# The last tile's second layer: from two interleaved halves to three parts in sequence, the middle one stored by ScalarE

## The chip, the core and the metric

The kernel runs on one core of one Trainium2 chip. The metric is the device time of one execution in microseconds, less is better. The profile names the engines PE (TensorE matmul), PEld (TensorE weight load), DVE (VectorE), ACT (ScalarE), POOL (GpSimd) and SP (SyncE). A name with a small q behind it (SPq, ACTq, PEldq) is that engine's sequencer, which issues DMAs, waits on semaphores and takes branches.

## What is computed

A sliding-window attention with four sink keys, followed by layer normalisation and a two-layer MLP with a residual. There are 4 sequences of 768 positions and 8 heads of 64, so that the MLP sees 3072 rows of 512 columns; its hidden layer has 2048 columns.

```python
scores = scale * np.matmul(q, k.transpose(0, 1, 3, 2))
keep = is_sink | in_window            # 4 sinks, window of 128
a = softmax(np.where(keep, scores, -1e9))
x = np.matmul(a, v)                   # heads side by side: 3072 x 512
xn = (x - mu) / np.sqrt(var + 1e-06) * g_ln
out = x + np.maximum(xn @ w_ch1, 0.0) @ w_ch2
```

## The kernel before

The 3072 rows are 24 tiles of 128 rows (`NT` = 24), and two tiles make a chunk (`NC` = 12 chunks). Attention is computed tile by tile; the MLP chunk by chunk, in `mlp(c)`. Its first layer makes 16 hidden blocks of 128 x 256 for the chunk: 8 PSUM banks' worth of matmuls on line 1045, each bank released by a ReLU on line 1055 that writes bf16 into `h`. The second layer takes the chunk's two tiles in turn (the loop over `i`, line 1061). For one tile it adds up 16 matmuls on line 1074 in one PSUM bank (`pc`): the stationary operand is a 128 x 128 block of `h`, the moving operand a block of `w2`. VectorE then multiplies the bank by the row's inverse deviation and adds `x` (line 1082, SCALAR_TENSOR_TENSOR, written to `ot`), and a DMA stores `ot` (line 1086).

Nothing in the code issues an instruction at once. `P.op(name, engines, priority, emit, ...)` puts each step in a plan with an estimated cost and a priority; `Plan.run` lays the steps out, taking on each engine, among those that can start first, the one of the lowest priority number (ties go to the one that was put in first). The steps are then emitted in the order of their planned start, and each engine works through its own in that order. So the priority on line 1078 sets the order of the matmul groups. The banks are a ring too: `pc` takes one of four single banks ("one").

Tile 23, the last, is cut into two halves of 256 columns (`parts` = 2, line 1065): each has its own bank, its own SCALAR_TENSOR_TENSOR and its own store. The groups of four matmuls have priorities `T + 4*i + s + 2*f + 0.5`: for the halves f = 0 and f = 1 these are 4.5, 5.5, 6.5, 7.5 and 6.5, 7.5, 8.5, 9.5 above T. So the first group of the second half goes between the third and the last group of the first half: the first half is complete after 20 matmuls, not 16.

Behind the last tile stands the end of the program. A flag made from the row sums has been written to SBUF (line 1120); each engine loads it into a register (line 1150, TENSOR_LOAD) and branches on it (line 1151, COMPARE_BRANCH) past the code of a general fallback, `general`, which is not run here. Then each engine reports with a DRAIN (line 1186), SP after it has waited for every store; when all have reported, GpSimd clears the semaphores, and the program ends.

Of the kernel before, what the change touches and what calls it, by code (L numbers as in the profile page):

```python
# [196 lines left out]
def pe(us):  # L197
    return {"PE": (us, us + Plan.PE_DRAIN)}


def act(n):
    t = 0.065 + 0.000833 * n
    return (t, t + 0.105)


def dve(n, per=1.04):
    t = 0.067 + 0.001 * per * n
    return (t, t + 0.09)
# [16 lines left out]
SW_Q = (0.25, 0.7, 0.9)  # L225

LOW, HIGH = 1e-9, 1e9
NEG = -1e30
NEVER = -1e9
BIG = 3.3e38  # L230
# [138 lines left out]
def kernel(  # L369
# [19 lines left out]
    DM = moe_w_ch1.shape[0]  # L389
# [3 lines left out]
    NT = B * RB  # L393
# [8 lines left out]
    P = Plan()  # L402
# [104 lines left out]
    def negs(e):  # L507
        V.tensor_scalar(neg[:, 0:5:2], upper.unsqueeze(1).to_broadcast([128, 3, 128]), -1.0, -NEG, op0=ALU.add, op1=ALU.mult)
        V.tensor_scalar(neg[:, 1:5:2], upper.unsqueeze(1).to_broadcast([128, 2, 128]), NEG, None, op0=ALU.mult)
        V.memset(neg[0:NS, 0:2], 0.0)  # L510
# [37 lines left out]
    for c in range(4):  # L548
        sl = slice(512 * c, 512 * (c + 1))
# [477 lines left out]
    def mlp(c):  # L1027
        T = 16.0 * c + 8.0
        xnt = xnt_b[c]
        h1 = []  # L1030
        by_tile = c < PAR["by_tile"]
        for u in range(NH1 // 2):
            ph, hb = Buf(f"ph{c}_{u}", "one"), Buf(f"h{c}_{u}", "h1")

            def mm_t(e, u=u, ph=ph):
                for s in range(4):
                    for j in range(NDM):
                        nc.tensor.matmul(ph.t[:, 128 * s:128 * s + 128], lhsT=w1[u // 2][:, j, 128 * s:128 * s + 128],  # L1038
                                         rhs=xnt.t[:, j, 128 * (u % 2):128 * (u % 2) + 128], start=j == 0, stop=j == NDM - 1)

            def mm(e, u=u, ph=ph):
                for s in range(2):
                    ht = 2 * u + s
                    for j in range(NDM):
                        nc.tensor.matmul(ph.t[:, 256 * s:256 * s + 256],  # L1045
                                         lhsT=w1[ht // 4][:, j, 128 * (ht % 4):128 * (ht % 4 + 1)],
                                         rhs=xnt.t[:, j, :], start=j == 0, stop=j == NDM - 1)
            pr = T + u + 0.5
            o = P.op(f"ph{c}_{u}", pe(0.944 if by_tile else 0.872), pr, mm_t if by_tile else mm, reads=[xnt_t[2 * c + u % 2] if by_tile else xnt, (Bw1 if c < PAR["x_by_dma"] else Bw1g)[u // 2]],
                     writes=[ph], hold=[hb, xnt])  # L1050
            last_use[u // 2] = [o]

            def rl(e, ph=ph, hb=hb):
                if e == "ACT":
                    nc.scalar.activation(hb.t, ph.t, AF.Relu)  # L1055
                else:
                    V.tensor_scalar_max(hb.t, ph.t, 0.0)
            P.op(f"rl{c}_{u}", {"ACT": act(512), "DVE": dve(512)}, pr - 3, rl, reads=[ph], writes=[hb])
            h1.append(hb)
        T += 8  # L1060
        for i in range(2):
            t = 2 * c + i
            b, r = t // RB, t % RB
            ot, st, rs, x = Buf(f"ot{t}", "ot"), xst_b[t], xst_b[t, "rs"], x_b[t]
            parts = 2 if t == NT - 1 else 1
            wd = DM // parts
            for f in range(parts):
                pc = Buf(f"pc{t}{f}", "one")
                sl = slice(wd * f, wd * (f + 1))
                for s in range(4):  # L1070
                    def mm(e, s=s, i=i, pc=pc, sl=sl, wd=wd):
                        for ii in range(4):
                            ht = 4 * s + ii
                            nc.tensor.matmul(pc.t[:, 0:wd],  # L1074
                                             lhsT=(h1[2 * s + i].t[:, 128 * ii:128 * ii + 128] if by_tile else
                                                   h1[ht // 2].t[:, 256 * (ht % 2) + 128 * i:256 * (ht % 2) + 128 * i + 128]),
                                             rhs=w2[s][:, ii, sl], start=ht == 0, stop=ht == NH1 - 1)
                    P.op(f"pc{t}{f}_{s}", pe(0.865 / parts), T + 4 * i + s + 2 * f + 0.5, mm,
                         reads=[*([h1[2 * s + i]] if by_tile else h1[2 * s:2 * s + 2]), Bw2[s]], **({"writes": [pc]} if s == 0 else {"rw": [pc]}))
                oo = Buf(f"oo{t}{f}")  # L1080
                P.op(f"o{t}{f}", {"DVE": dve(wd, 1.14)}, T + 4 * i + 3.5, lambda e, sl=sl, pc=pc, wd=wd, ot=ot, st=st, x=x:
                     V.scalar_tensor_tensor(ot.t[:, sl], in0=pc.t[:, 0:wd], scalar=st.t[:, 16:17],  # L1082
                                            in1=x.t[:, sl], op0=ALU.mult, op1=ALU.add),
                     reads=[pc, st, rs, x], writes=[ot, oo])
                P.op(f"st{t}{f}", {"SP": (0.54, 0.59)}, T + 4 * i + 3.6,
                     lambda e, sl=sl, ot=ot, b=b, r=r: (nc.sync if e == "SP" else nc.scalar).dma_start(
                         out[b, 128 * r:128 * (r + 1), sl], ot.t[:, sl]),
                     reads=[ot, oo], dma=HW_S)
# [13 lines left out]
    for c in range(NC):  # L1102
        mlp(c)
        if c == PAR["x_by_dma"] - 1:
            for s in range(4):
                for j in range(NDM):
                    P.op(f"w1g{s}{j}", {"DVE": fix(0.26), "ACT": act(512)}, 16.0 * c + PAR["w1g"] + 2 * s + 0.1 * j,
                         lambda e, s=s, j=j: V.tensor_scalar_mul(w1[s][:, j, :], w1[s][:, j, :], gt[:, j:j + 1]) if e == "DVE" else
                         nc.scalar.mul(w1[s][:, j, :], w1[s][:, j, :], gt[:, j:j + 1]),  # L1109
                         reads=[Bw1[s], Bc["gt"]], writes=[Bw1g[s]], after=last_use[s])  # L1110
# [15 lines left out]
    t = PAR["t0"]  # L1126
    for o in order:
# [6 lines left out]
        if n > 0:  # L1134
            free = [(max([e_ for b_, e_ in banks[i].lives if b_ < t], default=0.0), i) for i in range(8)
                    if all(e_ < t or b_ > o.start + 0.3 for b_, e_ in banks[i].lives)]
            if free:
                i = min(free)[1]
                sizes = [512] * (n // 2) + [256] * (n % 2) if cold else [256] * n
                items.append((t + 0.001, -1, (sizes, pairs[i // 2][:, i % 2, :] if i < 4 else ones[i - 4])))  # L1140
        t = o.start + occ * (2 if cold and not o.name.startswith("pm") else 1)
# [49 lines left out]
```

## Time and profile before

| what | value |
|---|---|
| runs | 216.91, 217.95 and 217.96 us, median 217.95 us |
| the profiled execution | 217.75 us, of which 216.3 us is the span from the first to the last instruction |
| granted TensorE clock, mean | 0.997 |
| PE busy | 95% of the span |
| last ReLU of the first layer ends | 205.28 us after the span's start |
| last three SCALAR_TENSOR_TENSOR start | 208.35, 210.65 and 211.86 us |
| last three stores issued by SP | 209.13, 211.16 and 212.37 us |

All times in profile rows count from the start of the span. 1.45 us of the profiled execution lie outside it. Of the span, 3.9 us lie behind the issue of the last store: in that stretch no engine computes.

### The profile page before, as it was taken

The numbers are of one execution on the slowest core, as the hardware profiler recorded it, in microseconds if no ns is written. First come the engines' busy times: TensorE is split into PE (matmuls) and PEld (weight loads), VectorE is DVE, ScalarE is ACT, GpSimd is POOL, SyncE is SP. The second block draws the span as 40 slices with busy tenths as digits, with TensorE's granted clock in tenths as the row PEclk, the third lists the DMA queues.
The fourth block names the chain that finished last, engine by engine and source line by source line (L and its number), as shares of the span: only waits on it lengthen the run. The fifth ranks groups of instructions, "written<-read, shape, count | busy, mean of one in ns | idle before, by whom it ended". The sixth has DMA issues, their size and how long they took to land.

```text
span 216.3 us, 6653 instructions
## 1 busy us (share of the span) xinstructions
PE 206.4 (95%) x2741; PEld 144.5 (67%) x2763; DVE 115.3 (53%) x315; ACT 110.1 (51%) x178; POOL 111.2 (51%) x166
## 2 busy tenths in 40 slices
PE   8898999999999999999999999999999999999991
PEld 2567875755865865865865865865856856856761
DVE  4689875698365356356266366266266266262021
ACT  3795497395652652652652652652652652622600
POOL 7978632499881980970970980971961021020000
PEclk9999999999999999999999999999999999999998
DMA  5999999999999899999998999999999202203011
GB/s 158 187 190 208 191 207 190 189 155 138 161 186 179 113 142 129 116 147 155 121 137 136 122 138 146 116 148 132 129 126 140 73 11 68 73 7 118 0 55 58
DMA packets 104557, 28.07 MB, mean 130 GB/s; under 512 B 94788, under 2 KB 101576, under 8 KB 104520
## 3 DMA queue, kind: packets, MB, share of 16 engines
q0 software_dynamic: 69872, 13.18, 87.5%
q1 hardware_dynamic: 33592, 13.87, 36.2%
q10 hardware_dynamic: 1056, 0.52, 0.9%
q8 instruction: 23, 0.38, 0.8%
q14 instruction: 14, 0.11, 0.2%
HBM read 27.43 MB, written 6.29 MB: 156 GB/s over the span
## 4 chain that ended last, share of the span: by engine, by line
PE 86%; DVE 5%; DMA 4%; issue 2%; ACT 1%; ACTq 0%; DVEq 0%
PE one L1074 37%; PE one L1045 36%; PE pair L979 3%; DMA natf<-in_q_dram 3%; DMA xnt<-xc 2%; PE one L952 2%; PE one L959 2%; PE one L968 1%; DVE st L880 1%; DVE xnt L908 1%; PE one L987 1%; PE one L1038 1%; DVE x L872 1%; PE pair L604 1%; PE pair L729 1%
## 5 line engine op out<-in xcount | busy, mean ns | idle before, releaser
L1074 PE MATMUL one<-w,h 128*128 128x512 bf16 (+1 forms) x378 | 84.5, 370 | 2.2 <-issue 1.4
L1055 ACT ACTIVATE h<-one 128x512 bf16<-128x512 f32 x93 | 55.6, 598 | 46.9 <-PE one L1045 42.6
L1045 PE MATMUL one<-xnt,w 128*128 128x256 bf16 x704 | 79.3, 273 | 0.0
L1045 PEld LDWEIGHTS <-w 128*128 128x128 bf16 x704 | 68.6, 98 | 10.4
L1074 PEld LDWEIGHTS <-h 128*128 128x128 bf16 x400 | 37.3, 98 | 39.6
L997 ACT ACTIVATE pe<-pair 128x768 bf16<-128x768 f32 x36 | 27.2, 808 | 41.0 <-PE pair L979 41.0
L644 POOL DMA_DIRECT2D vn<-in_v_dram x59 | 38.7, 701 | 9.2 <-DMA w<-in_moe_w_ch_dram 6.8
L889 POOL TENSOR_SCALAR st<-st 128x1 f32<-128x1 f32 x24 | 8.4, 350 | 63.5 <-DVE st L882 62.9
L1020 DVE RECIPROCAL rec<-one 128x4 f32<-128x4 f32 x36 | 6.4, 178 | 62.0 <-PE one L968 50.5
L1082 DVE SCALAR_TENSOR_TENSOR ot<-one,st,x 128x512 f32<-128x512 f32 (+1 forms) x25 | 18.2, 727 | 13.9 <-PE one L1074 9.0
L890 POOL TENSOR_TENSOR st<-st,mhalf 128x1 f32<-128x1 f32 x24 | 16.8, 701 | 2.0
L880 DVE BATCH_NORM_STATS2 st<-x 128x6 f32<-128x512 bf16 x24 | 16.7, 695 | 0.8
L702 POOL DMA_DIRECT2D nat<-in_k_dram x16 | 14.9, 934 | 2.6 <-DMA natp<-in_q_dram 1.5
L1022 DVE TENSOR_TENSOR x<-one,rec 128x256 bf16<-128x256 f32 x36 | 15.3, 424 | 1.2
L702 POOL DMA_DIRECT2D nat<-in_q_dram x16 | 14.3, 908 | 0.0
L1002 DVE TENSOR_TENSOR pe<-pe,band 128x768 bf16<-128x768 bf16 x24 | 12.3, 552 | 0.0
L884 DVE TENSOR_SCALAR xc<-x,st 128x512 bf16<-128x512 bf16 x24 | 8.9, 370 | 0.9
L979 PE MATMUL pair<-qT,kT 64*64 64x128 bf16 (+1 forms) x528 | 9.2, 204 | 0.0
L952 PEld LDWEIGHTS <-pe 128*128 128x128 bf16 (+1 forms) x144 | 6.2, 97 | 2.9 <-issue 0.8
L777 ACT ACTIVATE pe<-pair 128x1024 bf16<-128x1024 f32 (+1 forms) x8 | 7.1, 916 | 1.8 <-PE pair L729 1.4
L1038 PE MATMUL one<-xnt,w 128*128 128x128 bf16 x128 | 8.0, 219 | 0.0
L979 PEld LDWEIGHTS <-kT 64*64 64x64 bf16 x528 | 7.2, 108 | 0.4 <-ACT w L1109 0.4
(110 smaller groups left out, 167.0 us busy)
## 6 DMA issues: line engine op xcount, KB each, us to landing
out_dram<-ot SPq DMA_DIRECT2D x23, 256.0 KB
w<-in_moe_w_ch_dram POOLq DMA_DIRECT2D x8, 512.0 KB, 14.0
nat<-in_k_dram POOLq DMA_DIRECT2D x16, 128.0 KB, 4.6
nat<-in_q_dram POOLq DMA_DIRECT2D x16, 128.0 KB, 5.6
vn<-in_v_dram POOLq DMA_DIRECT2D x44, 32.0 KB, 6.0
vn<-in_v_dram POOLq DMA_DIRECT2D x15, 64.0 KB, 5.7
natp<-in_k_dram POOLq DMA_DIRECT2D x3, 256.0 KB, 6.5
vn<-in_v_dram POOLq DMA_DIRECT2D x6, 128.0 KB, 9.2
```

Source lines behind the costliest of these rows:

```text
L644: P.op(f"vld{t}_{i}", {"POOL": (0.8, 0.85)}, prio + 0.001 * i, lambda e, p0=p0, n=n, hs=hs, src=src: G.dma_start(m.t[p0:p0 + n, hs, 0:64], ...
L702: lambda e, nat=nat, ap=ap: G.dma_start(nat.t, ap), writes=[nat], dma=SW, after=gate(c))
L880: P.op(f"bn{t}", {"DVE": fix(0.60)}, d + 0.12, lambda e: V.bn_stats(st.t[:, 8:14], x.t), reads=[x], writes=[st, mv])
L890: G.tensor_tensor(st.t[:, 16:17], st.t[:, 17:18], mhalf, op=ALU.pow)),
L979: nc.tensor.matmul(pps[u].t[64 * g:64 * g + 64, h2, col + c0:col + c0 + n], lhsT=kt.t[rs, hp, k0:k0 + 64], rhs=qT.t[rs, hp, q0:q0 + n], st ...
L997: nc.scalar.activation(pes[j].t.rearrange("p a b -> p (a b)")[:, 0:768].rearrange("p (a b) -> p a b", a=2), pps[j].t[:, :, 0:384], AF.Exp, ...
L1002: V.tensor_mul(at_s, at_s, band[j] if r > 1 else edge[r][j].unsqueeze(1).to_broadcast([128, 4, 192]))
L1022: P.op(f"x{t - 1}{u}", {"DVE": dve(256)}, d + 0.051 + 0.002 * u, lambda e, u=u, rc=rc, pv=pv: V.tensor_tensor(x.t[:, 256 * u:256 * u + 256 ...
L1045: nc.tensor.matmul(ph.t[:, 256 * s:256 * s + 256], lhsT=w1[ht // 4][:, j, 128 * (ht % 4):128 * (ht % 4 + 1)], rhs=xnt.t[:, j, :], start=j ...
L1055: nc.scalar.activation(hb.t, ph.t, AF.Relu)
L1074: nc.tensor.matmul(pc.t[:, 0:wd], lhsT=(h1[2 * s + i].t[:, 128 * ii:128 * ii + 128] if by_tile else h1[ht // 2].t[:, 256 * (ht % 2) + 128 ...
L1082: V.scalar_tensor_tensor(ot.t[:, sl], in0=pc.t[:, 0:wd], scalar=st.t[:, 16:17], in1=x.t[:, sl], op0=ALU.mult, op1=ALU.add),
```

## The change

The last tile's 512 columns are cut at 256 and 384: three parts, of 256, 128 and 128 columns, each with its own bank, VectorE instruction and store. The groups get priorities that are four apart from part to part, so that the parts no longer interleave (4.5 to 7.5, 8.5 to 11.5, 12.5 to 15.5 above T), and planned costs that follow the width. The store of the part for which `len(cuts) - f` is 3 may only go to ScalarE: with four cuts that is f = 1, the middle part. Tiles 0 to 22 have two cuts and one part, for which that number is 2: they stay as they were, with SP as the only issuer.

```diff
+LAST_CUTS, LAST_ACT = (0, 256, 384, 512), (3,)
...
-            parts = 2 if t == NT - 1 else 1
-            wd = DM // parts
-            for f in range(parts):
-                pc = Buf(f"pc{t}{f}", "one")
-                sl = slice(wd * f, wd * (f + 1))
+            cuts = LAST_CUTS if t == NT - 1 else (0, DM)
+            for f in range(len(cuts) - 1):
+                pc, wd = Buf(f"pc{t}{f}", "one"), cuts[f + 1] - cuts[f]
+                sl = slice(cuts[f], cuts[f + 1])
...
-                    P.op(f"pc{t}{f}_{s}", pe(0.865 / parts), T + 4 * i + s + 2 * f + 0.5, mm,
+                    P.op(f"pc{t}{f}_{s}", pe(0.865 * wd / DM), T + 4 * i + s + 4 * f + 0.5, mm,
...
-                P.op(f"st{t}{f}", {"SP": (0.54, 0.59)}, T + 4 * i + 3.6,
+                P.op(f"st{t}{f}", {"ACT" if len(cuts) - f in LAST_ACT else "SP": (0.54, 0.59)}, T + 4 * i + 3.6,
```

## The prediction

> **What bounds the kernel now.** I read the page first, then the chain of waits over the last 26 us, then the timeline of the last 11 us, then the sequencers' instructions of lines 1150, 1151 and 1186, and last the DMA queues in short windows. From the page:
>
> ```profile
> PE 206.4 (95%) x2741; PEld 144.5 (67%) x2763; DVE 115.3 (53%) x315; ACT 110.1 (51%) x178; POOL 111.2 (51%) x166
> ```
>
> The kernel is a stream of matmuls, and the change doesn't touch it before the last tile. So only the tail counts. Its chain (start, duration, what) and its timeline:
>
> ```profile
> 197.59 6.99 PE one L1045 x64
> ...
> 211.86 0.48 DVE ot L1082
> ```
>
> ```profile
> 208.35 0.75 DVE L1082 SCALAR_TENSOR_TENSOR ot<-one,st,x 128x512 f32<-128x512 f32 x1 [2.61 <-PE one L1074]
> ...
> 210.65 0.48 DVE L1082 SCALAR_TENSOR_TENSOR ot<-one,st,x 128x256 f32<-128x256 f32 x1 [1.54 <-PE one L1074]
> ```
>
> ```profile
> 211.16 0.33 SPq L1086 DMA_DIRECT2D out_dram<-ot  x1
> ```
>
> ```profile
> 212.37 0.62 SPq L1086 DMA_DIRECT2D out_dram<-ot  x1
> ```
>
> VectorE follows PE at once, and the last store is issued 0.03 us after the last VectorE instruction (211.86 + 0.48 = 212.34). From there the span has 3.9 us left, and nothing in them computes. What they are is seen in the sequencers' rows (engine, instruction, count: duration in ns min/median/max, first to last start):
>
> ```profile
> L1150 ACTq TENSOR_LOAD <-flag x1: 472/472/472, 205.8 to 205.8; - x1
> ```
>
> ```profile
> L1150 PEldq TENSOR_LOAD <-flag x1: 748/748/748, 209.6 to 209.6; - x1
> ```
>
> ```profile
> L1151 ACTq COMPARE_BRANCH  x1: 50/50/50, 206.3 to 206.3; - x1
> ...
> L1151 ACTq EVENT_SEMAPHORE  x1: 17/17/17, 208.8 to 208.8; - x1
> ...
> L1151 PEldq COMPARE_BRANCH  x1: 3622/3622/3622, 210.5 to 210.5; - x1
> ...
> L1151 SPq COMPARE_BRANCH  x1: 58/58/58, 213.0 to 213.0; - x1
> ```
>
> ```profile
> L1186 POOLq EVENT_SEMAPHORE  x4: 17/17/17, 215.5 to 216.1; - x4
> ...
> L1186 SPq DRAIN  x3: 7/7/13, 215.4 to 215.7; - x3
> ...
> L1186 PEldq DRAIN  x2: 8/8/8, 214.3 to 215.8; - x2
> ```
>
> ```profile
> SPq L1186 <- DMA out_dram<-ot: 1.0, 1, 1.0
> ```
>
> The program ends when every engine has reported with its first DRAIN of line 1186. SP is last, at 215.4, after 1.0 us of waiting for a store; GpSimd goes on at 215.5 and the span ends at 216.3. The second to report is PE, at 214.3: its branch, taken at 210.5, holds it for 3.6 us. So whatever the store gains, the end comes forward by no more than 215.4 - 214.3 = 1.1 us unless PE's branch moves too. That is 0.5% of the kernel, about what a measurement of it can tell from no change.
>
> Why SP waits so long is in the DMA queues, in the windows 213.4 to 214.1 and 214.1 to 214.75 (queue: packets, MB, share of 16 engines):
>
> ```profile
> q1 hardware_dynamic: 135, 0.12, 51.0%
> q14 instruction: 1, 0.01, 5.4%
> ```
>
> ```profile
> q14 instruction: 1, 0.01, 4.5%
> q1 hardware_dynamic: 9, 0.01, 4.3%
> ```
>
> Most of the last store's packets are through by 214.1; a last nine (a sixteenth of 144) move only then, next to a code read on q14. I read this as one DMA engine's slice of the store standing behind the code that engines fetch after their branch.
>
> **The change part by part.** PE first. One matmul of 256 columns takes 6.99 / 64 = 0.109 us (line 1045 above). For 128 columns with a weight load each, line 1038 in the chain of waits has the price, and what PE still had before it when its sequencer loaded the flag is in the groups from 209.92 on:
>
> ```profile
> 25.29 1.79 PE one L1038 x32
> ```
>
> ```profile
> L1074 PE MATMUL one<-w,h 128*128 128x256 bf16 x17 | 2.0, 273 | 0.0
> ```
>
> 1.79 / 32 = 0.056 us. The tile costs 16 x 0.109 + 32 x 0.056 = 3.53 us in place of 32 x 0.109 = 3.49: +0.04. Counted from tile 22's VectorE start at 208.35, part one is complete at 210.10 (before: after 20 matmuls, 210.53, seen as 210.65 on VectorE), part two at 210.99, part three at 211.89 (before 211.86).
>
> The weak spot is the weight load:
>
> ```profile
> L1074 PEld LDWEIGHTS <-h 128*128 128x128 bf16 x49 | 4.7, 98 | 2.2
> ```
>
> A load lasts 98 ns, longer than a matmul of 128 columns; line 1038 has such a load for each matmul and still goes at 56 ns, so I take 56 and keep 98 as the upper bound (a rival). The Trainium skill, "TensorE: Matmul & The Clock Gate", section "Back-to-back issue gap", gives about 81 ns for a sustained stream of load and matmul pairs at 128 columns; by it the tile would cost 1.74 + 32 x 0.081 = 4.33 us, an estimate of 0.8 us more. Line 1038's stream disagrees with it.
>
> VectorE: 512 columns take 0.75 us and 256 take 0.48, so 1.04 ns a column; 128 take 0.48 - 0.13 = 0.35. Part two runs 210.99 to 211.34, part three 211.89 to 212.24. The last store is issued at 212.27, 0.10 earlier than now. The one more VectorE instruction lies in a gap of 0.73 us ahead of the last and costs nothing: were the gap gone, it would cost its 0.35.
>
> Stores. Part one's leaves SP at about 210.7 and is over long before. Part two's goes from ScalarE at 211.37. SP is free then (its issue would last 0.33, to 211.70, 0.57 before part three's), so the move saves nothing on SP's queue. The last store moves 64 KB in place of 128. Its 128 rows stay, each half as long; at 0.51 x 0.7 us x 16 / 135 = 42 ns for a packet of 1 KB and eight rows to an engine, halving can be worth between 0 and 0.17 us, and nothing while the slice behind the code read decides. I take 0.
>
> ScalarE's own price for an issue is in the timeline's first microseconds, 1.11 for two:
>
> ```profile
> 1.02 1.11 ACTq L666 DMA_DIRECT2D natf<-in_q_dram  x2
> ```
>
> ScalarE now waits for VectorE at 211.34 with its flag load and branch queued behind; nobody but GpSimd's last wait depends on these. Before, it had branched at 206.3 and was back at 208.8: 2.5 us, hidden. Now: issue 0.33 to 0.62 (SP's two prices, with ScalarE's 0.55 between them), flag load 0.47, branch at 212.2 to 212.5, back at 214.7 to 215.0, reported 0.1 later. The cover is SP's 215.4; it holds with 0.3 to spare. In that branch it also fetches code. The window 207 to 208 has nothing but two reads (40 slices of 25 ns, tenths of the DMA engines' time):
>
> ```profile
> DMA  0000000008009000000000000000000000000000
> ```
>
> ```profile
> q14 instruction: 2, 0.02, 4.9%
> ```
>
> They start at 207.23 and 207.30, 0.9 us behind the branches that ScalarE and GpSimd took at 206.3. ScalarE's read therefore moves to 213.1 to 213.4, where the last store's packets pass (now from 213.4 on, then from 213.3 on). So the slice that was late stays late. Bounds: if the read is in front, one more read of about half a microsecond, +0.5; if the store is ahead of all reads, the wait of 1.0 goes, to a floor that ScalarE and PE set. I take no change in the delay.
>
> PE's report. Its flag load started with 17 matmuls still to go. If what lets the sequencer run ahead is a number of queued instructions, then these 17 are now of 128 columns, and the load comes 17 x (0.109 - 0.056) = 0.90 later, plus the 0.04 of the stream: 210.5. PE then reports at 214.3 + 0.94 = 215.2. If it runs ahead by time, PE stays at 214.3. I take the number of instructions.
>
> The sum: reports at 215.3 (SP, 215.4 - 0.10), 215.2 (PE), 214.8 to 215.1 (ScalarE). The last is SP's, so the end moves by -0.10 us: span 216.2, profiled execution 217.75 - 0.10 = 217.65. The median of the runs stood 0.20 above the profiled one, so 217.85, rounded 217.8. The gain is small because two engines take the store's place within 0.5 us of it.
>
> **The rivals.** *Faster: the last store gets clear.* With an issue 0.10 earlier and rows half as long, all of its packets may be through before the code reads; then SP reports at about 214.4 (its wait of 1.0 gone). If PE runs ahead by time, ScalarE alone is the floor: 214.8 to 215.1, -0.3 to -0.6, 217.5. If by number, PE's 215.2 leaves -0.2. For it: the runs before lie 1.05 us apart (216.91 against 217.95), as they would if the slice is clear in some. Against it: ScalarE's read, which is new in just that place. Should ScalarE's branch not need its 2.5 us (SP's branch at 213.0 has less behind it), -1.1 is open, 216.85; with the scatter of the runs, down to 216.4.
>
> *Slower: one more block of code.* PE's instructions come in reads on q8, one for every so many. PE's weight loads between the last two such reads ahead of the branch, at 182.2 and 196.8, were:
>
> ```profile
> L1045 PEld LDWEIGHTS <-w 128*128 128x128 bf16 x64 | 6.3, 98 | 0.9
> L1074 PEld LDWEIGHTS <-h 128*128 128x128 bf16 x32 | 3.1, 98 | 3.6
> L952 PEld LDWEIGHTS <-pe 128*128 128x128 bf16 x8 | 0.4, 97 | 0.0
> L968 PEld LDWEIGHTS <-pe 64*64 64x64 bf16 x16 | 0.3, 107 | 0.0
> L959 PEld LDWEIGHTS <-ps 64*64 64x64 bf16 x4 | 0.1, 103 | 0.1
> ```
>
> These are 64 + 32 + 8 + 16 + 4 = 124 pairs of load and matmul. From 196.8 to the end there are 64 of line 1045, 49 of line 1074 and the flag's 2, 115 in all, and the change makes them 131. So a further read can come due at PE's flag load, just ahead of the read that the branch needs, on the same queue:
>
> ```profile
> q8 instruction: 1, 0.02, 3.7%
> ```
>
> In the window 211 to 213 one such read has 0.037 x 16 x 2 us = 1.2 us. If the branch's read must wait for it in full, PE reports at 215.2 + 1.2 = 216.4, +1.0: 218.95; if it is half done by then, +0.4; the middle is 218.65. It decides from 124 pairs on; the run-ahead of 17 pairs makes this a near thing, since the sequencer was just released from a wait when it met the earlier boundary. The Trainium skill, "Runtime: NRT & Kernel Launch", section "Instruction fetch mechanics", puts a block at 256 instructions and says that a taken branch out of the window fetches its page before going on; 256 is 128 pairs, so by it too 131 is past the boundary, by three.
>
> *Slower: weight loads bind.* If a load can't hide behind a matmul that is shorter than it, each pair takes the load's 98 ns: 32 x (98 - 56) = 1.35 us more, 219.2. It decides from the first matmul of part two. Line 1038 speaks against it. The Trainium skill's 81 ns (the section named above) is this rival at 218.65.
>
> *The change does not do what it says.* Were the parts still interleaved, part one would end late and nothing else move. But the priorities don't overlap, and of the four banks tile 22 and parts one and two hold three. I give it nothing of its own.
>
> **How the numbers follow.** Forecast (217.8; 217.5 to 218.1): 0.50. Faster rival: 0.25, over half of it more than 0.5% below 217.95 (216.86) because of the scatter: 0.14. One more block: 0.21, of which 0.08 is over 219.04, where the delays add up. Weight loads: 0.04, all of it above. With 0.02 on each side for the forecast's own scatter: faster 0.16, same 0.70, slower 0.14. The range 216.6 to 218.9 leaves out half of the faster rival's 0.14, 0.09 of the extra block and the 0.04: 0.20.
>
> **What would show it.** Right: VectorE's last three starts at 210.2, 211.0 and 211.9, the last 0.35 long; SP's last issue at 212.3; PE's flag load at 210.5 and its first DRAIN at 215.2; ScalarE's branch at 212.2 to 212.5 and its DRAIN at 214.8 to 215.1; SP's DRAIN at 215.3 after a wait for the store. Wrong: PE's flag load still at 209.6 (run-ahead by time); SP's wait for the store gone (faster rival); two q8 reads between 210.5 and 213 (one more block); the 32 matmuls of 128 columns taking more than 1.9 us.

## The result, and the profile after

| | before | after |
|---|---|---|
| runs | 22, median 217.93 us (216.71 to 218.55) | 22, median 218.46 us (217.96 to 219.37) |
| ratio of the times, after to before | | 1.0036, 95% interval 1.0022 to 1.005 |
| the profiled execution | 217.75 us, span 216.3 us | 218.07 us, span 216.6 us, granted clock 0.995 |

The change made the kernel slower, by about a third of a per cent. The forecast was 217.8 us, a little faster; 218.46 lies inside its range, on the other side. To read the medians one must know that the kernel before has two groups of times, here 8 runs from 216.71 to 217.16 us and 14 from 217.75 to 218.55 us, and that its profiled execution belongs to the upper one. The share of the groups differs from chip to chip, so that the median of before jumps between them. After has one group, and none of its runs is in the lower one of before. The means lie 0.82 us apart, the medians 0.53; what follows judges by the ratios and their intervals, and by the profiles.

Of the 0.32 us between the two profiled executions, 0.12 are there before the tail begins (VectorE's last 512-column instruction starts at 208.47 and not at 208.35). The tail itself makes 0.20.

The timeline of after shows the new tail as it was planned: VectorE's three parts, and ScalarE's issue 0.04 us behind the end of the first part of 128 columns.

```profile
208.47 0.75 DVE L1082 SCALAR_TENSOR_TENSOR ot<-one,st,x 128x512 f32<-128x512 f32 x1 [2.61 <-PE one L1074]
...
210.33 0.48 DVE L1082 SCALAR_TENSOR_TENSOR ot<-one,st,x 128x256 f32<-128x256 f32 x1 [1.11 <-PE one L1074]
...
211.12 0.35 DVE L1082 SCALAR_TENSOR_TENSOR ot<-one,st,x 128x128 f32<-128x128 f32 x1 [0.31 <-PE one L1074]
211.51 0.37 ACTq L1086 DMA_DIRECT2D out_dram<-ot  x1
211.95 0.35 DVE L1082 SCALAR_TENSOR_TENSOR ot<-one,st,x 128x128 f32<-128x128 f32 x1 [0.47 <-PE one L1074]
```

The sequencers' rows of after (engine, instruction, count: duration in ns min/median/max, first to last start) show what came of it:

```profile
L1150 PEldq TENSOR_LOAD <-flag x1: 485/485/485, 210.8 to 210.8; - x1
...
L1151 PEldq COMPARE_BRANCH  x1: 3938/3938/3938, 211.4 to 211.4; - x1
...
L1151 ACTq COMPARE_BRANCH  x1: 54/54/54, 212.5 to 212.5; - x1
...
L1151 ACTq EVENT_SEMAPHORE  x1: 17/17/17, 215.4 to 215.4; - x1
...
L1186 SPq DRAIN  x3: 7/7/13, 215.7 to 216.0; - x3
...
L1186 ACTq DRAIN  x2: 8/8/8, 215.5 to 216.0; - x2
...
L1186 PEldq DRAIN  x2: 8/8/8, 215.6 to 216.1; - x2
```

A report is the DRAIN with which an engine says that it is done. PE reports at 215.6 (before 214.3), ScalarE at 215.5 (before at 208.8, long ahead of everyone), SP at 215.7 (before 215.4). The store's end is no longer the one late thing: three engines end within 0.2 us.

SP's new lateness is not the store's. By the trace the last store's semaphore came at 215.17, against 215.28 before. Behind that, in the rows of SP between landing and report, stand these waits, first of after, then of before:

```profile
L1186 SPq EVENT_SEMAPHORE  x8: 28/28/28, 215.2 to 215.6; - x8
```

```profile
L1186 SPq EVENT_SEMAPHORE  x1: 28/28/28, 215.3 to 215.3; - x1
```

SP waits for eight DMA semaphores in a fixed order, and the DMAs take these semaphores in turn. Before, the last store had the last of the eight. With one DMA more it has the first, and seven waits follow, some 0.06 us each: (215.6 - 215.2) / 7.

The last two of these waits ask for more than a DMA. In the trace's records the last but one also takes a semaphore that PE raises when it is back from its branch, and the last one a semaphore of ScalarE. So SP's report always comes behind PE's and ScalarE's returns. In this execution both were back at 215.47, and SP, which came to these two waits at 215.54 and 215.61, did not have to wait for them.

The last slice still ends late, beside code reads. In the window 213.6 to 215.2 the DMA queues of after have two reads on q14, the last nine packets of SP's store (q1) and the last seven of ScalarE's (q10).

```profile
q14 instruction: 2, 0.02, 4.2%
...
q1 hardware_dynamic: 9, 0.00, 2.2%
...
q10 hardware_dynamic: 7, 0.00, 1.9%
```

### The profile page after: what moved, and what is told of

It reads as the page before. It is cut to its first block, busy times and chain, and to the rows that moved or that the text cites. A ratio compares the mean times of both kernels' runs of the same rounds, so it can differ in the third digit from the quotient of the medians.

```text
span 216.6 us, 6710 instructions
## 1 busy us (share of the span) xinstructions
PE 208.2 (96%) x2779; PEld 144.5 (67%) x2779; DVE 115.0 (53%) x316; ACT 110.0 (51%) x178; POOL 111.4 (51%) x166
## 4 chain that ended last, share of the span: by engine, by line
PE 89%; DVE 3%; DMA 3%; ACT 1%; issue 1%; ACTq 0%; DVEq 0%
PE one L1074 39%; PE one L1046 36%; PE pair L980 3%; DMA natf<-in_q_dram 3%; PE one L953 2%; PE one L960 2%; PE one L969 1%; PE one L988 1%; PE one L1039 1%; ACT pe L778 1%; PE pair L730 1%; PE pair L751 1%; DVE st L881 1%; DVE x L873 1%; DVE xnt L909 1%
## 5 line engine op out<-in xcount | busy, mean ns | idle before, releaser
L1074 PE MATMUL one<-w,h 128*128 128x512 bf16 (+2 forms) x416 | 87.4, 363 | 0.0
L1082 DVE SCALAR_TENSOR_TENSOR ot<-one,st,x 128x512 f32<-128x512 f32 (+2 forms) x26 | 18.4, 708 | 13.5 <-PE one L1074 8.6
```

What stands on the lines that cost most here:

```text
L1074: nc.tensor.matmul(pc.t[:, 0:wd], lhsT=(h1[2 * s + i].t[:, 128 * ii:128 * ii + 128] if by_tile else h1[ht // 2].t[:, 256 * (ht % 2) + 128 ...
```

## The experiments

The theory: the end waits for the last of three reports, and the change made all three late, PE's by its narrow matmuls, ScalarE's by its store, SP's by one DMA more. The rivals: the narrow matmuls' code alone (one more block to read); ScalarE's part alone; the waits alone. The table gives the first DRAIN of line 1186 on PE and ScalarE, and SP's second one, which raises the same semaphore as the others' first and stands 0.07 us behind SP's own first. The times are in us behind the start of VectorE's last 512-column instruction, called the reference instant (208.35 before, 208.47 after), so that starts that differ don't count. Each is of one profiled execution. A dash: no issue by ScalarE in that kernel, and its report is early. Since SP waits for the other two, its report is the last in every row; the other two columns tell whether it had to wait for them.

| kernel | median us | ratio to before (95%) | SP | PE | ScalarE |
|---|---|---|---|---|---|
| before | 217.93 | 1 | 7.07 | 5.97 | - |
| after | 218.46 | 1.0036 (1.0022 to 1.005) | 7.27 | 7.10 | 7.06 |
| e1, sequence alone | 216.74 | 0.9977 (0.9956 to 0.9997) | 5.86 | 5.69 | - |
| e6, sequence and narrow matmuls | 218.31 | 1.0025 (1.0008 to 1.0042) | 7.49 | 7.38 | - |
| e7, sequence and ScalarE's store | 217.01 | 0.9976 (0.9957 to 0.9995) | 6.09 | 5.81 | 6.02 |
| e5, before and one DMA more | 218.28 | 1.0024 (0.9991 to 1.0056) | 6.32 | 5.82 | - |
| e2, after, all stores by SP | 218.69 | 1.0039 (1.002 to 1.0059) | 7.72 | 7.17 | - |
| e3, after, eight DMAs more in all | 218.66 | 1.0042 (1.0023 to 1.0062) | 7.59 | 7.39 | 7.52 |
| e8, wide part last, all by SP | 217.67 | 0.9985 (0.9964 to 1.0006) | 7.05 | 6.94 | - |
| e9, wide part last, middle by ScalarE | 217.93 | 1.001 (0.9988 to 1.0031) | 7.01 | 6.72 | 6.35 |
| e12, e8 with code blocks shifted | 216.91 | 0.999 (0.9962 to 1.0019) | 6.02 | 5.91 | - |
| e11, after with code blocks shifted | 218.29 | 1.0059 (1.0035 to 1.0082) | 7.53 | 6.88 | 7.46 |
| e10, before, first half by ScalarE | 217.27 | 1.0006 (0.9985 to 1.0027) | 6.61 | 5.90 | 6.54 |
| after once more, beside e10 to e12 | 218.56 | 1.0068 (1.0041 to 1.0095) | 7.57 | 7.08 | 7.50 |

Three sets ran, each beside its own runs of before: e1, e5, e6, e7 (before 217.87); e2, e3, e8, e9 (218.04); e10, e11, e12 and after (217.12). Medians are compared within a set; where two sets are compared, the text says so. The lower group of before lies at 216.5 to 217.2 us in all three.

### The change in its three parts

**e1, halves in sequence, nothing else.**

```diff
-P.op(f"pc{t}{f}_{s}", pe(0.865 / parts), T + 4 * i + s + 2 * f + 0.5, mm,
+P.op(f"pc{t}{f}_{s}", pe(0.865 / parts), T + 4 * i + s + 4 * f + 0.5, mm,
```

> Two halves of 256 columns as before, but in sequence (4*f in the priority), both stores on SP. Theory (the end waits for the last of three reports, of SP, PE and ScalarE; the changed kernel has made all three late): none of the three moves here. PE's flag load stays some 1.8 us ahead of PE's last matmul, SP's last store has the last of the semaphores that SP waits on, ScalarE branches at 206. Ratio to before 0.998 to 1.002, median 217.9. Rival A (only ScalarE's new code read delays the last store): the same, 217.9. Rival B (doing the parts in sequence is what costs): 218.4.

The median is 216.74, where 217.9 was expected. All twelve runs lie between 216.51 and 217.38: the upper group of before, 18 of its 35 runs in this set, is gone. Its sequencer rows:

```profile
L1186 SPq DRAIN  x3: 7/7/13, 214.3 to 214.6; - x3
...
L1186 PEldq DRAIN  x2: 8/8/8, 214.2 to 214.7; - x2
```

SP's wait for the last store (1.0 us before) is not among its waits from 213 on any more. The one left is for PE, at the meeting of the engines behind SP's report, and it was there before too:

```profile
SPq L1186 <- PEq L1186: 0.7, 2, 0.5
```

So the order of the halves, which the prediction gave no value, is worth 0.23% (0.03 to 0.44%), and alone it beats the kernel before, by little but clear of the interval's end.

**e6, the narrow matmuls alone.** To e1 are added the second half's matmuls as 32 of 128 columns, into the same bank, with one VectorE instruction and one store, all stores by SP.

```diff
+n_sub = 2 if f == 1 else 1
+ws = wd // n_sub
+for g, s in [(g, s) for g in range(n_sub) for s in range(4)]:
+    def mm(e, s=s, i=i, pc=pc, c0=ws * g, sk=slice(sl.start + ws * g, sl.start + ws * (g + 1)), ws=ws):
...
-            nc.tensor.matmul(pc.t[:, 0:wd],
+            nc.tensor.matmul(pc.t[:, c0:c0 + ws],
...
-                             rhs=w2[s][:, ii, sl], start=ht == 0, stop=ht == NH1 - 1)
+                             rhs=w2[s][:, ii, sk], start=ht == 0, stop=ht == NH1 - 1)
```

> PE's part alone: halves in sequence, and the second half's matmuls are 32 of 128 columns in place of 16 of 256, into the same bank, with one VectorE instruction and one store on SP as before. Theory: PE's flag load moves 0.9 to 1.0 us later (to about 210.7) because some 17 pairs are queued behind PE whatever their width; PE reports at 215.4 instead of 214.3, so that no run can end as early as the fastest before (217.0 and less): median 218.0, ratio 1.001 to 1.003. Rival A (ScalarE's code read): store and ScalarE are as before, ratio 1.000. Rival B (sequence): as the run with two plain halves in sequence.

218.31 against e1's 216.74: in the same set the narrow matmuls alone cost 1.57 us, which is more than e1 gains (1.13 at the medians) and, by the ratios, which are of two sets, nearly all that the change loses (1.0025 and 1.0036). Its rows (line numbers are two further on):

```profile
L1152 PEldq TENSOR_LOAD <-flag x1: 485/485/485, 210.6 to 210.6; - x1
...
L1153 PEldq COMPARE_BRANCH  x1: 4292/4292/4292, 211.2 to 211.2; - x1
...
L1188 SPq DRAIN  x3: 7/7/13, 215.7 to 216.0; - x3
...
L1188 PEldq DRAIN  x2: 8/8/8, 215.7 to 216.1; - x2
```

PE's flag load comes 2.29 us behind the reference instant, as in after; in before and e1 it is 1.29. The load itself takes 0.49 us and not 0.75, so that the branch is taken 0.73 us later. And the branch takes 4.29 us, where e1's took 3.34 and before's 3.62. One likely reason for the longer branch is in the DMA queues from 210.6 to 213, two reads of code on q8 and not one:

```profile
q8 instruction: 2, 0.03, 8.3%
```

It can't be all: the first profile of after has one read there, and its branch still takes 3.94 us. So the 1.57 us hold the later flag load and a longer branch together, and no run has e6 without the second read; the nearest is e11, below. SP is late in e6 because it waits for PE, not for the store:

```profile
SPq L1188 <- PEq L1153: 1.6, 1, 1.6
```

**e7, ScalarE's store alone.** To e1 is added that the first half's store goes from ScalarE.

```diff
-P.op(f"st{t}{f}", {"SP": (0.54, 0.59)}, T + 4 * i + 3.6,
+P.op(f"st{t}{f}", {"ACT" if parts == 2 and f == 0 else "SP": (0.54, 0.59)}, T + 4 * i + 3.6,
```

> ScalarE's part alone: halves in sequence, 256 columns each, the first half's store on ScalarE, as many DMAs as before. Theory: ScalarE's branch moves to 211.7, its code read to 212.6, it reports at 214.3 to 214.8, below the SP report of 215.4 of a slow store, but above PE's 214.3: median 217.9, ratio 1.000 to 1.002. Rival A: the code read keeps the last store's slice in every run, median 218.4, ratio 1.003.

The median is 217.01, where 217.9 was expected, against e1's 216.74; the ratios of the two to before can't be told apart. ScalarE is back from its branch 2.6 us after it was taken, and SP, which has waited 0.2 us for it, reports with it:

```profile
L1151 ACTq COMPARE_BRANCH  x1: 54/54/54, 211.7 to 211.7; - x1
...
L1151 ACTq EVENT_SEMAPHORE  x1: 17/17/17, 214.3 to 214.3; - x1
...
L1186 SPq DRAIN  x3: 7/7/13, 214.4 to 214.7; - x3
...
L1186 ACTq DRAIN  x2: 8/8/8, 214.4 to 214.7; - x2
```

An issue by ScalarE at the end costs little as long as it comes early enough: 0.2 us in SP's report, 0.27 at the median.

**e5, one DMA more alone.** Before, with tile 20's store in two pieces; this is well before the tail and moves only the turn of the semaphores.

```diff
+PIECES = {20: 2}
...
+n_st = PIECES.get(t, 1)
...
+for k in range(n_st):
+    sk = slice(edges[k], edges[k + 1])
```

> The number of DMAs alone: the kernel before with tile 20's store cut in two, 20 us ahead of the end, so that the last store's semaphore is the first of the eight that SP waits on and no longer the last. Theory: SP has seven waits of 0.06 us left when the last store lands, so it reports 0.43 us later: 218.35 where the store is late, less where it is not; ratio 1.001 to 1.002. Rivals A and B: ratio 1.000.

Both groups of before are there, each moved up: four runs at 217.24 to 217.45 (before's lower group 216.58 to 217.2), the others from 218.22 (before's upper group from 217.87). In SP's rows the eight waits and then the report, 0.5 us after the landing:

```profile
L1191 SPq EVENT_SEMAPHORE  x8: 28/28/28, 214.5 to 214.9; - x8
...
L1191 SPq DRAIN  x1: 13/13/13, 215.0 to 215.0; - x1
```

The ratio's interval still holds 1; the price of about 0.45 us rests on the groups and on these rows.

### Undoing one part of the change

**e2, the middle store by SP.**

```diff
-LAST_CUTS, LAST_ACT = (0, 256, 384, 512), (3,)
+LAST_CUTS, LAST_ACT = (0, 256, 384, 512), ()
```

> The changed kernel (256, 128, 128) with the middle store on SP too. Theory: ScalarE's report is early again, but PE's stays 7.1 us behind tile 22's VectorE instruction and SP still has its seven waits: 217.9 to 218.3. Rival A: 217.0 to 217.4.

The median is 218.69, above the 217.9 to 218.3 expected, and the ratio is no better than the change's own. ScalarE is out of it, but SP now pays for it in its issues, first in e2, then in after:

```profile
L1086 SPq DMA_DIRECT2D out_dram<-ot x4: 332/726/1676, 209.2 to 212.7; - x4
```

```profile
L1086 SPq DMA_DIRECT2D out_dram<-ot x3: 332/333/336, 209.2 to 212.3; - x3
...
L1086 ACTq DMA_DIRECT2D out_dram<-ot x1: 374/374/374, 211.5 to 211.5; - x1
```

An issue that mostly takes 0.33 us took 1.1 and 1.7 us here. Each of the two began while one of PE's code reads on q8 was under way and the store ahead on SP's queue was not through, and ended 0.37 to 0.39 us behind the end of that read, as the issue of 0.62 us in before did. With the store ahead out of the way, an issue during such a read takes 0.33 (after, e7, e10, e12). But in e8 and e9 both conditions hold and the issue takes 0.33 too, so what holds an issue up is not settled. SP's report comes 0.45 us later than in the first profile of after (7.72 and 7.27); e2's trace also has a second read on q8, which that one lacks. Taking the store off ScalarE gains nothing.

**e3, the last store back on the last semaphore.** After, with the stores of tiles 19, 20 and 21 in 4, 3 and 3 pieces, seven DMAs more, so that the turn is the same as before.

```diff
+PIECES = {19: 4, 20: 3, 21: 3}
```

> The changed kernel with its ScalarE store, and the stores of tiles 19, 20 and 21 in 4, 3 and 3 pieces, so that the last store has the last semaphore of SP's list. Theory: SP reports 0.4 us earlier, but PE's and ScalarE's reports stay at 7.1: 218.0 to 218.3. If the seven waits alone made the loss: 217.6 to 218.0 with runs near 217.0.

No gain: 218.66, above the 218.0 to 218.3 expected. Three reports stand together, and taking seven waits from SP moves nothing, since SP then waits for PE, and 0.1 us more for ScalarE (line 1186 is 1191 here):

```profile
L1191 SPq DRAIN  x3: 7/7/12, 216.0 to 216.3; - x3
...
L1191 ACTq DRAIN  x2: 8/8/8, 216.0 to 216.3; - x2
...
L1191 PEldq DRAIN  x2: 8/8/8, 215.9 to 216.4; - x2
```

### The narrow parts first

**e9 and e8.** With cuts at 128 and 256 the last part is wide, and PE's queue ends in matmuls of 256 columns. e9 is after with these cuts; e8 also has all stores by SP and e3's pieces. The lines show e9's edit.

```diff
-LAST_CUTS, LAST_ACT = (0, 256, 384, 512), (3,)
+LAST_CUTS, LAST_ACT = (0, 128, 256, 512), (3,)
```

> The changed kernel with the widths in another order: parts of 128, 128 and 256 columns in sequence, the middle one stored by ScalarE, as many DMAs and instructions as the changed kernel. Theory (three late reports, PE's most): the 17 matmuls behind PE's flag load are of 256 columns again, so PE loads the flag 1.29 us behind tile 22's last VectorE instruction (2.29 in the changed kernel) and reports 1.2 us earlier; ScalarE's store is issued 1 us earlier; what is left is the seven waits of SP, 0.45: 217.2 to 217.4. Rival A (ScalarE's code read delays the last store): 218.0 to 218.5. Rival C (three parts, four stores or narrow matmuls cost by themselves): 218.4.

> As the run before (parts of 128, 128, 256), but all stores on SP, and the stores of tiles 19, 20 and 21 cut into 4, 3 and 3 pieces, seven DMAs more, so that the last store has the last semaphore of SP's list again. Theory: all three reports are where the two plain halves in sequence have them (216.74 us): 216.7 to 217.0. Rival C: 218.0 or more.

Both missed: 217.93 and 217.67. PE's flag load came back to 1.44 us as expected, but its branch grew, in e8 to

```profile
L1156 PEldq COMPARE_BRANCH  x1: 4442/4442/4442, 210.6 to 210.6; - x1
```

and in e9 to 4.20 us, with two reads on q8 in each, as in e6. The reading is that sixteen more pairs of load and matmul had put a border between blocks of code just ahead of the branch; the next run tests it. In e8 SP waits 1.2 us for PE. In e9 it does not wait for PE: its last store lands 6.43 us behind the reference instant, and the seven waits follow.

**e12 and e11, the border moved.** The warm-up matmuls at the start of the kernel, whose results nothing uses, are cut to 128 columns and issued in larger number: 48 PE instructions more in the first 16 us. e12 is e8 with that, e11 is after with that.

```diff
-sizes = [512] * (n // 2) + [256] * (n % 2) if cold else [256] * n
+sizes = [128] * (2 * n)
```

> Parts of 128, 128 and 256 columns, all stores on SP, last semaphore kept (as the run of 217.67), with the same shift of PE's code blocks. Theory with the extra block: all reports are back where the two plain halves in sequence have them, PE's branch takes 3.4 to 3.9 us in place of 4.4: 216.7 to 217.0. If three parts cost by themselves: 217.6.

> The changed kernel with PE's idle-time matmuls of the first 16 us cut into 128 columns (24 pairs of load and matmul more, the same PE time in a stretch in which PE waits anyway), which moves PE's code blocks by 48 instructions: the extra block of code is then read 1.3 us earlier and is over when PE branches. Theory with the extra block (it doubles the code read of PE's branch in most runs of the changed kernel): PE's branch takes 3.4 to 3.9 us, it reports at 7.1 behind tile 22's VectorE instruction, 217.9 to 218.2. If the extra block costs nothing: as the changed kernel, 218.3 to 218.7.

e12's median, 216.91, is as expected. Its branch, and the code read by PE between 210.5 and 213.5:

```profile
L1156 PEldq COMPARE_BRANCH  x1: 3401/3401/3401, 211.7 to 211.7; - x1
```

```profile
q8 instruction: 1, 0.02, 1.9%
```

(In this execution all instants are about 0.5 us later than in the others at 130 us and 1 us at the end; the differences are what counts.) The other read on q8 comes at 209.0, ahead of PE's flag load. The reports go from 7.05 to 6.02 us, the medians, across two sets, from 217.67 to 216.91: the extra block costs e8 about 1.0 us in its profile and 0.8 by the medians. The ratios to before, 0.9985 and 0.999, don't show it, since before itself had 27 of 35 runs above 217.5 us in e8's set and 11 of 29 in e12's. In after the same shift gives little: 218.29 against 218.56 in the same set, ratios not told apart. There PE reports at 6.88, but SP waits 0.5 us for ScalarE, which is as late without the block (7.46) as with it (7.50 in the next run).

**After once more**, unchanged, in that set:

> The changed kernel once more, for a second profile (its first, 218.07, was among its shortest executions). Theory with the extra block: two reads of PE's code between 2.5 and 4.2 us behind tile 22's VectorE instruction, PE's branch 4.1 to 4.3 us long, 218.4 to 218.6. Without it: one read, 3.9 us, and the time still 218.4.

It has the second read on q8 that the first profile of after lacks (window 210.9 to 213.1, first of this execution, then of the first one), and a ScalarE that comes back 3.4 us after its branch where the first took 3.0:

```profile
q8 instruction: 2, 0.03, 7.3%
```

```profile
q8 instruction: 1, 0.02, 3.4%
```

```profile
L1151 ACTq COMPARE_BRANCH  x1: 54/54/54, 212.6 to 212.6; - x1
...
L1151 ACTq EVENT_SEMAPHORE  x1: 17/17/17, 216.0 to 216.0; - x1
...
L1186 SPq DRAIN  x3: 7/7/13, 216.1 to 216.4; - x3
```

```profile
SPq L1186 <- ACTq L1151: 0.3, 1, 0.3
```

Here SP waits for ScalarE. PE's report has not moved: its branch takes 3.99 us with the second read and 3.94 without, and the report comes at 7.08 and 7.10. This execution took 218.58 us, the first 218.07, which is among the shortest of after's 22. The median, 218.46, is nearer to this one.

### Why before has two groups

**e10, before with the first half's store by ScalarE**, the halves still interleaved (e7's edit without e1's).

> The kernel before (halves interleaved) with the first half's store on ScalarE in place of SP. It asks why two halves in sequence lose the late runs of the kernel before (218.0 beside 216.9). Theory: in the late runs the first half's store still has a slice waiting behind PE's code read in SP's queue when SP issues the last store (issue of 0.62 in place of 0.33 us), so that the last store starts late and falls behind the next code reads; with the first half in ScalarE's queue the last issue takes 0.33 and there are no runs at 217.8 or above: 216.9 to 217.3. If the late runs come from somewhere else: two groups again, 216.9 and 218.0.

Eleven of twelve runs lie between 217.11 and 217.56, as expected; the one at 218.73 has the lowest granted clock of the twelve, 0.992. In this set 11 of before's 29 runs stand above 217.5, so twelve runs alone say little. In before, SP's three issues and their longest, then the same lines of e10:

```profile
L1086 SPq DMA_DIRECT2D out_dram<-ot x3: 332/337/622, 209.1 to 212.4; - x3
```

```profile
L1086 SPq DMA_DIRECT2D out_dram<-ot x2: 333/335/337, 209.0 to 212.2; - x2
...
L1086 ACTq DMA_DIRECT2D out_dram<-ot x1: 373/373/373, 211.0 to 211.0; - x1
```

The 0.62 us of the last issue goes to 0.337 when the first half's store is on another queue, and the last store's data are through by 213.8 where a slice of before's ran on to 214.65. The reading that fits: in before the first half's store, late because of the interleaving, meets PE's code read; SP's next issue is held, and the last store comes too late to be ahead of the code reads of the engines that branch. In e1 the first half is sent 0.4 us earlier. A slice of it ends late too, but PE's read ends just as SP issues the last store; that issue takes 0.33 us and the store is through by 213.8. That the held issue makes the upper group is an inference from these profiles, one of each kernel. e10 pays at ScalarE (report at 6.54, and SP waits for it), and its ratio is 1.

## Why the prediction was wrong, point by point

The step that failed is the sum of the three reports. It had SP at 215.3, PE at 215.2 and ScalarE at 214.8 to 215.1, so that SP would end 0.10 us earlier. Measured were 215.7, 215.6 and 215.5 in the first profile of after, and 216.1, 215.6 and 216.1 in the second, whose tail begins 0.1 us later. What the engines do up to their branches was foreseen well; what comes behind the branches was not, as follows.

**Right, with sizes.** The matmuls: the chain of after has

```profile
205.68 6.24 PE one L1074 x60
```

60 matmuls in 6.24 us; before, 44 in 6.20. The 32 narrow ones stand in place of 16 wide ones of 0.109 us and cost 0.04 us more in all: (16 x 0.109 + 0.04) / 32 = 56 ns each. The 98 ns of a load don't hold in this stream. Nor do the 81 ns of the Trainium skill ("TensorE: Matmul & The Clock Gate", "Back-to-back issue gap"). VectorE's starts (210.33, 211.12, 211.95; 210.2, 211.0 and 211.9 were given, and after starts 0.12 later), its 0.35 us, SP's last issue at 212.3, ScalarE's branch at 212.5 at the late end of 212.2 to 212.5. The run-ahead of PE's sequencer goes by a number of queued instructions: in all fourteen traces 17 matmuls start behind the start of the flag load, whatever their width. The load moved by 1.00 us (0.94 given), in e6 too, and came back to 1.44 when the last 16 matmuls were wide. The bound of 1.1 us on any gain was PE's, and e1 shows it as the floor: there SP ends 0.2 us behind PE.

**Mis-sized: PE's report.** The later flag load was carried over to the report as it was. In fact the load got shorter (0.49 us for 0.75), the branch came 0.73 us later, and it took 3.94 us in place of 3.62. PE reported 1.13 us later by the reference instant, where 0.94 were given. Why the branch takes longer with one read in front of it is not settled.

**Wrong: what stands behind the last store on SP.** The sum took 0.10 us off SP's report. The store did land 0.10 earlier, but the extra DMA was costed by its issue alone and not by its turn on the semaphores. In e5 the turn is worth 0.45 us, and in the first profile of after it is what SP's report, 215.7 in place of 215.3, stands behind. In the change it adds little to the time all the same: SP's report is 0.11 us behind PE's wherever SP waits for PE (e6, e8, e12), so PE at 7.10 would have held it to 7.21, and it was 7.27. e3 takes the turn away and gains nothing.

**Wrong: ScalarE's cover.** The cover "holds with 0.3 to spare" rested on a return of 2.5 us, read from a branch that had only one other engine's read beside its own. At 212.5 it took 3.0 us, once more 3.4, and 3.4 and 3.5 in e11 and e3. With earlier branches it took 2.6 us in e7 (211.7), 2.7 in e10 (212.0) and 3.1 in e9 (211.5). Why it differs so is not settled; no run took the other engines' reads away. Nor is it so that "nobody but GpSimd's last wait depends on these": SP's last wait does, by 0.3 us in the second profile of after and 0.5 in e11.

**Wrong: that ScalarE's issue saves nothing on SP's queue.** The gap there was worked out with an issue of 0.33 us. In e2, where SP issues all four, two of them took 1.1 and 1.7 us. ScalarE's queue is no sure cure: in e3, which has it, SP's last issue took 0.61 us.

**Mis-sized: the chance of one more block of code (0.21).** The working put 131 pairs against 124 and called it near. It happened in e6, e2, e3, e8, e9 and in the second profile of after, not in the first. Its price in the prediction, 0.4 to 1.0 us, fits e8 and e12 (0.8 to 1.0). The Trainium skill's rule ("Runtime: NRT & Kernel Launch", "Instruction fetch mechanics"), blocks of 256 instructions, that is 128 pairs, spoke for the block at 131. Of the seven traces with these sixteen pairs more, six have the second read; the first one of after, with one, does not. In the change itself the block adds little: PE reports at 7.08 with it, at 7.10 without it and at 6.88 in e11, and ScalarE binds as well.

**Wrong: the sum was made against one group of before.** The profiled execution, at 217.75, was of the upper group, where SP waits 1.0 us for a store. The spread of 1.05 us was noted, but used only for a gain. SP waits for PE, so a change that makes PE report 1.1 us later forbids the lower group for good, whatever the store does, and that is most of the loss: from about 217.0 to 218.4 for the runs that would have been in it (8 of 22), about 0.5 for the others. The order of the parts was a second term put at nothing: halves in sequence free the last store, which the faster rival wanted from narrower rows. e1 has that gain, and e6 shows that the narrow matmuls give back more than it.

That before's lower group is the case without the long wait is read from e1, e5 and e10; no execution of before in that group was profiled.

## What to carry to other kernels

At the end of a kernel price every engine's last report (its flag load, its branch, the code it reads, the waits that follow the last DMA's own), not the last store alone: bringing the store forward gains only what the next engine leaves, 1.1 us here. Narrow instructions at the end of a queue make what is queued behind them late, since the run-ahead is counted in instructions: 17 matmuls here. If a tail must be cut, put the narrow parts first; here that took 0.85 us off PE's flag load, though no version in three parts beat the kernel before by its ratio. And look at whether the times of a kernel form groups before taking one profile as its base: here the smallest edit, the sequence alone (0.9977 of before, 0.9956 to 0.9997), is as good as any, and e7 is not told apart from it.

## What the runs showed of the hardware

- A store's issue on SP took 0.33 us in most cases, but 0.62 (before), 1.12 and 1.68 us (e2) when it began during one of PE's code reads with the store ahead not yet through; it then ended 0.37 to 0.39 us behind the read. In e8 and e9 the same conditions held and the issue took 0.33. ScalarE's issues took 0.37 each.
- SP's final waits are served in a fixed order and cost 0.06 us each even when there is nothing left to wait for: one DMA more, far ahead of the end, moved both groups of before by about 0.45 us (e5). The last two also wait for PE's and ScalarE's return from their branches (1.6 us for PE in e6, 0.3 for ScalarE in the second profile of after).
- PE's flag load, the next instruction of its sequencer behind the matmuls, started when 17 matmuls were still to start, in all fourteen traces and for both widths.
- Sixteen more pairs of load and matmul put one more read of code ahead of PE's branch, which then took 4.4 us (e8; e1 without the pairs 3.3). Forty-eight more instructions at the start of the kernel moved that read ahead of the flag load, and the branch took 3.4 us again (e12).
